# Retention attention and an ELU feed-forward layer: all steps of every engine in a new written order

## The chip, the cores and the metric

The kernel runs on one core of a Trainium2 chip. The core has a matrix engine (TensorE, PE in the profile, with its weight loads in a row of their own, PEld), a vector engine (VectorE, DVE), a scalar engine (ScalarE, ACT), a general engine (GpSimd, POOL) and a queue engine (SyncE, SP), and 16 DMA engines that move data between the chip's memory (HBM) and the core's buffer (SBUF). TensorE writes its results to a small accumulation buffer (PSUM), from which VectorE and ScalarE read. Each engine runs its own instruction list in the order written, and waits on semaphores for what it needs from the others.

The metric is device time in microseconds (us) for one execution, as the median of some runs. A profile is one execution with a recorder beside it; its span is the time between its first and last instruction.

## The reference, cut to what matters

Four batches, eight heads, 768 positions, 64 features for each head; `x` has 3072 tokens of 512 features and the hidden layer has 2048.

```python
for b in range(12):                        # blocks of 64 positions, one after the other
    intra = (qb @ kb^T) * Dmask            # Dmask[i,j] = lam^(i-j) for i >= j, else 0
    intra = intra @ vb
    inter = (qb * lam^(pos+1)) @ kv_state
    out[block] = intra + inter
    kv_state = lam^64 * kv_state + (kb * lam^(63-pos))^T @ vb
h = x @ w_in                               # x: the attention's output, heads side by side
g = where(h > 0, h, exp(min(h, 0)) - 1)
return g @ w_out
```

Inputs and output are fp32; products take fp16 operands and gather in fp32.

## The kernel before, in words

**Tiling.** Work is cut into 24 attention *steps*: step s is block s//2 of the batch pair 2*(s%2) (`where`, L50), that is 128 tokens and eight heads. Steps s and s+2 belong to the same pair of batches, so the state of step s is needed by step s+2. Two steps make a *group* of 256 tokens, of which there are 12; a group's attention output `xt` goes through the feed-forward layer.

**One attention step** on TensorE consists of small products of 64x64 operands, which `visit` (L295) issues in a block: the transposes T of k and q (`mm_T`; for the first steps in another form), the scores S (`mm_S`, into `psZ`), the state update U (`mm_U`, into the other half of `psZ`), the inter part I (`mm_I`, the state with the decayed q) and the intra part O (`mm_O`, masked scores with v). One call of `visit(so, us, ss, sx)` can take O of step `so`, U of `us`, S of `ss` and T of `sx`. Around it the other engines do: `att_C` (L233), the copy of the transposes from PSUM to the tile `T`; `att_P` (L225), the scores times the mask, on VectorE; `att_N` (L273), the new state; `att_X` (L262), the copy of the output to `xt`. Three *decays* prepare operands: `decay_v` (L189, tile `vd`, v by a factor for each row), `decay_s` (L198, tile `sd`, the state by its factor) and `decay_q` (L216, tile `qs`, the transposed q by a factor for each column). Each reads and writes SBUF alone, so VectorE or GpSimd can run it; `decay_s` has a form for ScalarE, too. From step 10 on, `dma_T` (L251) lets the DMA transpose k and q on SP's queue into a tile `TD` of two buffers, so that TensorE needn't.

**The feed-forward layer.** `mm1_h` (L420) is a part of the first product, into one of two PSUM banks `psH` (tag `h`). Two forms of the ELU follow: `mm1_e` (L435) with Exp and Relu on ScalarE and then `mm1_g` (L443) on VectorE, or, for later groups, `elu` (L463) with Relu and Exp on ScalarE one after the other and VectorE reading `psH` once more. The second product of steps 0 to 5 is plain (`mm2`, L490; `mm2_o`, L500, copies and stores); for groups from 3 on it is done with seven smaller products instead of eight (`part`, L559, and `product_of`), with sums of the weights (`w_sum`, L515), sums of g (`g_sum`, L525), and copies and additions of the results (`keep` L578, `add` L583, `c2` L587, `store` L568).

**Loads.** k, q and v come in on GpSimd's DMA queue (`load`, L71), which turns fp32 into fp16 on the way, into 12 buffers each. The issue of such a load is an instruction of GpSimd, and stands in one line with its decays. `wi` (four tiles, `load_wi` L97, two halves each) and `wo` (four, `load_wo` L110) come on the same queue. The second half of `wi2` waits for a semaphore, `crossed`, which TensorE raises after its first inter part. k and q of step 0 come raw as fp32 on other queues (`kraw`, `qraw`) and are cast by `cast0` (L177).

**What sets the order.** Nothing is scheduled by a planner: the pools run under a manual schedule, and every engine has its instructions in the order in which the program writes them. The order is written in three parts: loads ahead of the constants (L130 to L136); the string `start` (L631), whose words are a letter for a function and its arguments (`H0.0.1.0` calls `mm1_h(0, 0, 1, 0)`, `A4.4.5.6` calls `visit(4, 4, 5, 6)`, `R` issues all the later loads up to step 11); and, for groups from 3 on, a loop over eight parts u of each group (L670 to L752) with a tail (L754 to L780). In the loop a part is: one `mm1_h`, then at u of 0 and 4 the next loads, at u of 1 and 5 two decays and one `visit`, then one of the seven products, sums, and the ELU.

## Time and profile before

| what | value |
|---|---|
| time, median of 3 runs | 206.41 us (205.39 to 207.72) |
| profiled execution: span | 204.2 us |
| instructions in the span | 7590 |
| PE (TensorE matmuls) | 189.6 us busy |
| PEld (its weight loads) | 156.6 us busy |
| DVE (VectorE) | 168.7 us busy, 279 instructions |
| ACT (ScalarE) | 146.5 us busy, 283 instructions |
| POOL (GpSimd) | 123.4 us busy, 174 instructions |
| DMA | 24.36 MB in 94194 packets, mean 119 GB/s |

The page gives the span alone; the profiled execution's own time is taken to be what the span and the launch around it make, and 206.41 - 204.2 = 2.2 us is what lies between the span of this one execution and the median of the three.

How to read it: the page gives for each engine the busy time, its share of the span and the number of instructions. A view by stretch gives the same for pieces of the span. A timeline lists instructions by start, each with its start and its length in us, its engine, line, operation, the tile that it writes and those that it reads (`out<-in`), the shapes, and in brackets the idle time before it with what ended it. Groups of instructions carry a count (x22), and three numbers, least, median and largest ns of one. Rows named `POOLq` or `SPq` are issues of a DMA on that engine's queue.

### The profile page before, as it was taken

How to read it: one execution, taken by the hardware profiler on the slowest of the kernel's cores; microseconds unless marked ns; L12 is line 12 of the kernel's file. 1: busy time of each engine (PE TensorE's matmuls, PEld its weight loads, DVE VectorE, ACT ScalarE, POOL GpSimd, SP SyncE). 2: the span in 40 equal slices, each digit the busy share in tenths (PEclk: the TensorE clock that was granted, in tenths of full speed). 3: DMA queues.
4: the chain of work that ended last, by engine and by line, in shares of the span. 5: the costliest groups of instructions: out<-in, count | busy, mean ns of one | idle time of the engine just before them, and what ended most of it. 6: DMA issues, size and time to landing. Idle time of an engine off the chain costs nothing.

```text
span 204.2 us, 7590 instructions
## 1 busy us (share of the span) xinstructions
PE 189.6 (93%) x3216; PEld 156.6 (77%) x3216; DVE 168.7 (83%) x279; ACT 146.5 (72%) x283; POOL 123.4 (60%) x174
## 2 busy tenths in 40 slices
PE   0679899999999999999999989999999999999991
PEld 0457777647777777888888878888888888888881
DVE  4776996489989998999989999989979866758672
ACT  5626987635774879999878677788688788876820
POOL 8977832598998959997709999999222200020000
PEclk9999999999999999999999999999999999999998
DMA  6999999999999999999999999999915404004043
GB/s 102 157 171 171 152 206 196 180 124 156 117 148 150 173 108 172 153 134 78 74 163 109 206 105 86 185 111 105 169 27 69 94 0 108 0 6 100 3 103 103
DMA packets 94194, 24.36 MB, mean 119 GB/s; under 512 B 86160, under 2 KB 91152, under 8 KB 94160
## 3 DMA queue, kind: packets, MB, share of 16 engines
q0 software_dynamic: 73744, 13.64, 94.7%
q1 hardware_dynamic: 19968, 9.77, 26.9%
q10 hardware_dynamic: 448, 0.46, 1.0%
q8 instruction: 25, 0.41, 0.9%
q14 instruction: 9, 0.07, 0.1%
HBM read 27.27 MB, written 6.29 MB: 164 GB/s over the span
## 4 chain that ended last, share of the span: by engine, by line
PE 85%; DVE 4%; DMA 3%; POOL 3%; issue 2%; ACT 1%; POOLq 0%; DVEq 0%
PE psH L428 40%; PE psM L551 23%; PE psM L495 10%; DMA wi<-in_moe_w_in_dram 3%; PE psO_None L328 2%; POOL vn L79 1%; PE psZ L352 1%; PE psO_None L337 1%; PE psHB L551 1%; PE psHA L551 1%; DVE s L533 1%; PE psZ L344 1%; DVE g L475 1%; POOL kn L79 1%; PE psO L359 1%
## 5 line engine op out<-in xcount | busy, mean ns | idle before, releaser
L428 PE MATMUL psH<-xt,wi 128*128 128x256 f16 (+1 forms) x896 | 100.1, 261 | 1.9 <-ACT e L438 0.6
L428 PEld LDWEIGHTS <-wi 128*128 128x128 f16 x896 | 78.2, 100 | 13.3 <-issue 2.1
L475 DVE SCALAR_TENSOR_TENSOR g<-e,psH 128x512 f16<-128x512 f32 x58 | 39.6, 683 | 14.3 <-ACT e L474 13.8
L472 ACT ACTIVATE r<-psH 128x512 f32<-128x512 f32 x58 | 34.7, 598 | 18.3 <-PE psH L428 18.2
L474 ACT ACTIVATE e<-r 128x512 f32<-128x512 f32 x58 | 36.5, 630 | 1.8
L79 POOL DMA_DIRECT2D kn<-in_k_dram x46 | 32.2, 720 | 9.2 <-DMA wo<-in_moe_w_out_dram 5.1
L79 POOL DMA_DIRECT2D vn<-in_v_dram x48 | 34.1, 741 | 2.0 <-DMA wi<-in_moe_w_in_dram 1.1
L438 ACT ACTIVATE e<-psH 128x512 f32<-128x512 f32 x38 | 22.8, 601 | 14.7 <-PE psH L428 14.4
L551 PEld LDWEIGHTS <-s 128*128 128x128 f16 x288 | 28.1, 98 | 3.3
L445 DVE SCALAR_TENSOR_TENSOR g<-e,r 128x512 f16<-128x512 f32 x38 | 25.7, 685 | 4.1 <-ACT r L440 4.0
L220 POOL TENSOR_TENSOR qs<-TD,powi 128x512 f16<-128x512 f16 x11 | 13.9, 1264 | 19.3 <-PE psO_None L328 13.1
L79 POOL DMA_DIRECT2D qn<-in_q_dram x36 | 25.3, 735 | 0.0
L551 PE MATMUL psM<-wt,s 128*128 128x256 f16 x192 | 24.9, 273 | 0.0
L495 PE MATMUL psM<-wo,g 128*128 128x512 f16 x96 | 24.0, 379 | 0.0
L440 ACT ACTIVATE r<-psH 128x512 f16<-128x512 f32 x38 | 22.9, 602 | 0.0
L551 PEld LDWEIGHTS <-g 128*128 128x128 f16 x216 | 20.6, 98 | 2.6
L193 DVE TENSOR_TENSOR vd<-vn,rev 128x512 f16<-128x512 f16 x22 | 17.2, 783 | 1.8 <-DMA vn<-in_v_dram 1.7
L228 DVE TENSOR_TENSOR P<-psZ,mask 128x512 f16<-128x512 f32 x24 | 16.4, 684 | 2.0 <-PE psZ L344 1.1
L551 PE MATMUL psM<-wo,g 128*128 128x256 f16 x136 | 17.6, 272 | 0.0
L495 PEld LDWEIGHTS <-g 128*128 128x128 f16 x96 | 8.7, 98 | 7.0
L570 POOL DMA_DIRECT2D out_dram<-o x2 | 1.1, 574 | 21.1 <-DVE o L585 21.1
L533 DVE TENSOR_TENSOR s<-g 128x1024 f16<-128x1024 f16 x18 | 13.8, 764 | 0.0
(85 smaller groups left out, 228.7 us busy)
## 6 DMA issues: line engine op xcount, KB each, us to landing
out_dram<-o SPq DMA_DIRECT2D x43, 128.0 KB, 3.3
vn<-in_v_dram POOLq DMA_DIRECT2D x48, 64.0 KB, 5.0
kn<-in_k_dram POOLq DMA_DIRECT2D x46, 64.0 KB, 4.3
qn<-in_q_dram POOLq DMA_DIRECT2D x36, 64.0 KB, 4.5
wi<-in_moe_w_in_dram POOLq DMA_DIRECT2D x8, 256.0 KB, 8.9
wo<-in_moe_w_out_dram POOLq DMA_DIRECT2D x4, 512.0 KB, 12.6
qn<-in_q_dram POOLq DMA_DIRECT2D x5, 128.0 KB, 5.3
kraw<-in_k_dram SPq DMA_DIRECT2D x2, 128.0 KB, 4.7
```

Source lines behind the costliest of these rows:

```text
L79: nc.gpsimd.dma_start(out=keep[s][half(r)], in_=src[b + r, :, c * L : (c + 1) * L, :].rearrange("h p d -> p h d"),)
L193: eng.tensor_tensor(out=st[s]["vd"][:], in0=vn[s][:], in1=rev[:].unsqueeze(2).broadcast_to([128, H, D]), op=ALU.mult,)
L228: nc.vector.tensor_tensor(out=d["P"][:].rearrange("p y j t -> p y (j t)"), in0=psS, in1=mask[:].rearrange("p y j t -> p y (j t)"), op=ALU. ...
L428: nc.tensor.matmul(psH[:, i, :], lhsT=wi[n // 4][:, kk, (n % 4) * 128 : (n % 4 + 1) * 128], rhs=xt[grp][:, kk, c0 * 128 : c0 * 128 + T], s ...
L438: nc.scalar.activation(e[:], psH[:], AF.Exp)
L440: nc.scalar.activation(r[:], psH[:], AF.Relu)
L445: nc.vector.scalar_tensor_tensor(out=place(grp, c0, nc_, n0, nb, step), in0=e[:], scalar=-1.0, in1=r[:], op0=ALU.add, op1=ALU.min,)
L472: nc.scalar.activation(r[:], psH[:], AF.Relu, scale=-1.0)
L474: nc.scalar.activation(e[:], r[:], AF.Exp, scale=-1.0)
L475: nc.vector.scalar_tensor_tensor(out=place(grp, 0, 2, u, 2, NF2), in0=e[:], scalar=-1.0, in1=psH[:], op0=ALU.add, op1=ALU.max,)
L495: nc.tensor.matmul(acc[s], lhsT=g_of(s, n), rhs=wo[n // 4][:, n % 4, :], start=(n == 0), stop=(n == NFT - 1),)
L551: nc.tensor.matmul(to, lhsT=lhsT, rhs=rhs, start=start and n == 0, stop=stop and n == NF2 - 1, skip_group_check=True,)
```

## The change

No product, no load and no store is added or taken away. All that is written in three parts before, the loads, `start`, and the loop with its tail, now stands in one string `plan`, in a new order; so each engine's list is in a new order, GpSimd's loads and SP's transposes and stores among it. What else differs:

- words can end in a flag that names the engine. With it, `decay_v` and `decay_s` and `decay_q` (`V`, `D`, `Q`) run on GpSimd instead of VectorE: 30 decays in all, against 19 before. `mm1_e`/`elu_e` (`E`, `e`) take the Relu (or the minimum with 0) on VectorE instead of ScalarE, and `att_X`, `keep` and `mm2_o` copy on VectorE; `att_C` can copy k on ScalarE or q on VectorE.
- `elu` is cut in two words, `e` (Relu and Exp) and `g` (VectorE's combination), which can stand apart.
- the second half of `wi2` no longer waits for `crossed`. TensorE still raises it.
- the loads stand each at its own place (`l`, `w`, `y`), q1 and k1 first; q3 stands ahead of the first `wi`, q4 and k4 ahead of the last `wo`; the stores (`o`) too, one of them (`o18.5`) on GpSimd's queue.
- k of step 0 is cast ahead of q (`Fk Fq`), and the mask product (`K0`) stands later.
- which of the two banks `M` a plain second product takes is listed (`BANK`).

```diff
+    plan = (
+        "Fk Fq A...0 C0.1.1 lq1 lk1 lv0 lv1 K1 A..0. lq3 w0.0 V0 A.0.. A...1 K0 w0.1 lv2 lk2 lq2 "
+        "V1 lk3 P0 C1 A0... A..1. P1 X0 H0.0.1.0 E0.0.1.0 N0 A.1.. w1.1 V2 w1.0 D2 G0.0.1.0 N1 "
+        "A1... X1 A...2 C2.1 H0.1.1.0 D3 E0.1.1.0 A.2.2. A...3 C3.1 H0.0.2.4 Q2 lv3 P2 lq4 w2.0 "
+        "w2.1 lk4 V3.1 y0 G0.1.1.0 I2 A2... N2 Q3.1 X2.1 E0.0.2.4 H0.0.2.6 A.3.3. w3.1 w3.0 y1 "
+        "E0.0.2.6.1 y2 P3 H1.0.1.0 E1.0.1.0.1 H1.0.1.4 I3 y3 G0.0.2.6 E1.0.1.4.1 A3... G1.0.1.4 "
+        "X3 H1.0.1.8 E1.0.1.8.1 H0.0.2.8 E0.0.2.8 A...4 H0.0.2.10 H1.1.1.4 M1.0 G1.0.1.0 "
+        "E1.1.1.4 C4.0.1 A..4. M0.0 lq5 lk5 H0.0.2.14 G0.0.2.8 G1.0.1.8 H0.0.2.12 H1.1.1.0 lv4 "
+        "E0.0.2.10.1 G0.0.2.4 H1.0.2.12 M1.4 M0.4 G0.0.2.10 E0.0.2.14.1 H1.0.2.14 E0.0.2.12.1 "
+        "B1.1 G0.0.2.14 E1.1.1.0 G1.1.1.0 H1.1.1.8 lq6 M0.8 G0.0.2.12 Q4 E1.0.2.12 B1.0 M1.8 "
+        "M1.12 N3 D4 E1.1.1.8.1 M0.12 Z1 P4 B2.0 G1.1.1.8 B4.0 V4 Z0 G1.1.1.4 M2.0 E1.0.2.14.1 "
+        "A...5 M3.0 M2.4 C5 Q5 G1.0.2.12 lk6 lk7 A4.4.5.6 X4 B2.1 G1.0.2.14 M3.4 N4 lq7 lv5 lv6 "
+        "V5 H2.0.1.4 M3.8 E2.0.1.4 G2.0.1.4 P5 C6.1 H2.0.1.12 H2.0.1.8 V6 A5.5.6.7 lk8 M3.12 "
+        "M2.8 X5 P6 H2.1.1.4 H2.0.1.0 E2.0.1.8.1 M2.12 D6 B3.1 H2.1.1.12 Q6 lv7 lk9 H2.1.1.8 V7 "
+        "E2.0.1.12 C7 E2.1.1.4 lk10 lq8 lq9 D5 lv9 lq10 T10 N5 E2.0.1.0 Z2 E2.1.1.8 G2.0.1.0 "
+        "A6.6.7.8 M4.0 E2.1.1.12 G2.0.1.8 D7 P7 H2.1.1.0 B4.1 N6 C8.1 Q7 Z3 lv8 G2.0.1.12 M4.4 "
+        "M4.8 A7.7.8.9 lv10 lv12 X6 Q8 M4.12 E2.1.1.0 X7 h3.0 h3.1 C9.1 G2.1.1.4 G2.1.1.8 "
+        "G2.1.1.12 Z4 G2.1.1.0 N7 M5.0 M5.4 h3.4 h3.2 P8 V8 A8.8.9. h3.5 h3.7 lv11 M5.8 lk11 "
+        "D9.1 lq13 Q9 e3.1 g3.1 e3.0 h3.3 lq11 lk12 D8 e3.4 g3.0 V9 g3.4 lq14 lq12 P9 N8 "
+        "A9.9.10. e3.2 e3.5 X8 g3.2 V10.1 B3.0 lk14 T11 D10 T12 h3.6 lv14 lk13 lk18 M5.12 e3.7 "
+        "e3.3 V11.1 Q11.1 N9 T13 X9 P10 g3.7 lv13 e3.6 Q10 lk15 V14.1 h4.2 e4.2 g3.5 h4.4 g3.6 "
...
+        "o19.0 k10.u2 s10.3 h11.7 g11.5 p10.7 e11.6.1 e11.7 k10.c45.1 p10.3 g11.6 g11.7 j p11.1 "
+        "p11.4 k11.u1 s11.1 a10.2 p11.5 o20.0 s11.2 p11.6 s11.3 p11.2 k11.c45 c10 o21.0 k11.u2 "
+        "p11.7 s11.4 a11.3 o22.1 c11 o23.3 o18.5 p11.3 a11.2 o22.2 "
+    )
...
-            if (i, c) == (2, 1):
-
-                ins.wait_op(crossed, 1, "sem-ge")
...
+    def copy(eng, out, in_):
+        if eng is nc.scalar:
+            nc.scalar.copy(out=out, in_=in_)
+        else:
+            eng.tensor_copy(out, in_)
...
-    def mm1_e(grp, c0, nc_, n0):
+    def mm1_e(grp, c0, nc_, n0, on_dve=0):
         psH, nb, T, name = unit[grp, c0, nc_, n0]
         e = msb.tile([128, nb, T], FP32, tag="e", bufs=4, name=f"e{name}")
         nc.scalar.activation(e[:], psH[:], AF.Exp)
         r = msb.tile([128, nb, T], FP16, tag="r", bufs=4, name=f"r{name}")
-        nc.scalar.activation(r[:], psH[:], AF.Relu)
+        if on_dve:
+            nc.vector.tensor_scalar_max(r[:], psH[:], 0.0)
+        else:
+            nc.scalar.activation(r[:], psH[:], AF.Relu)
         unit[grp, c0, nc_, n0] = (e, r, nb, T, name)
...
-    def elu(grp, u):
-
+    def sbuf_form(grp, u):
+        return grp == 3 or grp == 4 and u < 6
+
+    def elu_e(grp, u, on_dve=0):
+
+        if sbuf_form(grp, u):
+            mm1_e(grp, 0, 2, u, on_dve)
+            return
         psH, nb, T, name = unit[grp, 0, 2, u]
-        if grp == 3 or grp == 4 and u < 6:
-            mm1_e(grp, 0, 2, u)
+        r = msb.tile([128, nb, T], FP32, tag="r", bufs=4, name=f"r{name}")
+        if on_dve:
+            nc.vector.tensor_scalar_min(r[:], psH[:], 0.0)
+        else:
+            nc.scalar.activation(r[:], psH[:], AF.Relu, scale=-1.0)
+        e = msb.tile([128, nb, T], FP32, tag="e", bufs=4, name=f"e{name}")
+        nc.scalar.activation(e[:], r[:], AF.Exp, scale=1.0 if on_dve else -1.0)
+        unit[grp, 0, 2, u] = (psH, e)
+
+    def elu_g(grp, u):
+        if sbuf_form(grp, u):
             mm1_g(grp, 0, 2, u, NF2)
             return
-
-        r = msb.tile([128, nb, T], FP32, tag="r", bufs=4, name=f"r{name}")
-        nc.scalar.activation(r[:], psH[:], AF.Relu, scale=-1.0)
-        e = msb.tile([128, nb, T], FP32, tag="e", bufs=4, name=f"e{name}")
-        nc.scalar.activation(e[:], r[:], AF.Exp, scale=-1.0)
+        psH, e = unit.pop((grp, 0, 2, u))
...
-    nacc = [0]
+    BANK = (1, 0, 0, 1, 0, 1)
...
+    def store(s, how):
+        cols = {1: lo, 2: hi}.get(how, slice(0, DM))
+        queues = {2: (nc.scalar, nc.sync), 3: (nc.sync, nc.scalar), 5: (nc.gpsimd,) * 2}.get(how, (nc.sync,) * 2)
         for r in range(2):
-            queues[r].dma_start(out=rows(s, r)[:, cols], in_=o[half(r), cols])
+            queues[r].dma_start(out=rows(s, r)[:, cols], in_=res[s // 2][s % 2][half(r), cols])
...
-    def later_loads():
-        load_wi(2, [1])
...
-    start = (
-        "Fq K0 Fk V0 A...0 C0 A.0.. K1 A..0. P0 A...1 N0 C1 A0... X0 V1 A..1. P1 A.1.. A1... X1 "
-        "N1 D2 H0.0.1.0 D3 E0.0.1.0 A...2 V2 C2 Q2 H0.1.1.0 A.2.2. I2 R P2 E0.1.1.0 A2... "
...
-    for grp in range(3, NG):
-        old, new = grp - 2, grp - 1
-        for u in range(8):
-            mm1_h(grp, 0, 2, u, NF2)
-            s = 2 * grp + 2 + u // 4
...
     steps = {
-        "I": lambda s: visit(s, None, None, None, True), "C": att_C, "P": att_P, "X": lambda s: att_X(s, nc.scalar),
-        "Y": lambda s: att_X(s, nc.vector), "N": att_N, "D": lambda s: decay_s(s, eng=nc.vector), "L": load_step,
-        "V": lambda s: decay_v(s, nc.vector if s < 99 else nc.gpsimd),
-        "Q": lambda s: decay_q(s, nc.vector if s < 10 else nc.gpsimd),
...
+        "I": lambda s: visit(s, None, None, None, True), "C": att_C, "P": att_P,
+        "X": lambda s, e=0: att_X(s, nc.vector if e else nc.scalar), "N": att_N, "D": lambda s, e=0: decay_s(s, eng=by(e)),
+        "d": lambda s, a, b: decay_s(s, range(a, b)), "V": lambda s, e=0: decay_v(s, by(e)),
+        "Q": lambda s, e=0: decay_q(s, by(e)), "H": mm1_h, "E": mm1_e, "G": mm1_g, "M": mm2, "Z": mm2_o,
+        "K": consts, "B": w_sum, "T": dma_T, "h": lambda g, u: mm1_h(g, 0, 2, u, NF2), "e": elu_e,
+        "g": elu_g, "s": g_sum, "p": part_of, "a": sums, "c": c2, "o": store,
     }
...
```

The words of `plan` that stand beside `start`'s: `l` a load, `w` a half of `wi`, `y` a quarter of `wo`; `h`, `e`, `g` the first product and its ELU for groups from 3 on; `p` one of the seven products, `s` a sum of g, `k` a copy out of a bank, `a` and `c` additions, `o` a store, `j` the two last banks, `d` a `decay_s` on ScalarE.

More of the change, by code (lines that the diff above doesn't have):

```diff
@@ L114, in load_wo @@
         )
+    loads = {
+        "l": lambda a: load(a[0], int(a[1:])), "w": lambda a: load_wi(*map(int, a.split("."))),
+        "y": lambda a: load_wo(int(a)),
+    }
     ij = cst.tile([128, L], I32, name="ij")
@@ L267, in att_X @@
         O = st[s].pop("O").rearrange("p r (y t) -> p r y t", y=NHP)
-        if eng is nc.scalar:
-            nc.scalar.copy(out=to, in_=O)
-        else:
-            eng.tensor_copy(to, O)
+        copy(eng, to, O)
     def att_N(s):
```

224 lines of the change are left out of this document (56 added, 168 removed), and 40 rows, old and new, of tables (plan, start).

## The prediction

> **What bounds the kernel now.** I read the page first: the busy shares and the chain that ended last.
>
> ```profile
> span 204.2 us, 7590 instructions
> ...
> PE 189.6 (93%) x3216; PEld 156.6 (77%) x3216; DVE 168.7 (83%) x279; ACT 146.5 (72%) x283; POOL 123.4 (60%) x174
> ...
> PE 85%; DVE 4%; DMA 3%; POOL 3%; issue 2%; ACT 1%; POOLq 0%; DVEq 0%
> ```
>
> TensorE (PE) holds 85% of the chain. The change leaves every matmul in place and only reorders, so it can win no more than PE's idle time. Where is that? The next view gives busy time by stretch (the columns are PE, PEld, DVE, ACT, POOL, granted clock, DMA share, GB/s; the first number after the stretch is its length).
>
> ```profile
> 6.00:13.20 7.20, 4.64 (x136) 3.50 (x136) 5.95 (x11) 3.30 (x10) 6.00 (x10) 1.00 1.61 160
> 13.20:30.00 16.80, 15.64 (x301) 13.34 (x302) 13.73 (x24) 11.58 (x23) 11.32 (x17) 1.00 1.34 175
> 30.00:60.00 30.00, 29.70 (x582) 20.81 (x580) 24.16 (x40) 19.25 (x36) 22.51 (x35) 1.00 1.55 154
> 60.00:90.00 30.00, 30.00 (x566) 23.25 (x565) 29.27 (x48) 24.03 (x51) 27.23 (x40) 1.00 2.14 149
> 90.00:118.00 28.00, 28.00 (x485) 24.45 (x484) 25.59 (x42) 23.27 (x46) 20.41 (x27) 1.00 1.53 126
> 118.00:123.00 5.00, 4.47 (x41) 3.71 (x39) 5.00 (x6) 3.73 (x7) 5.00 (x6) 1.00 1.38 105
> 123.00:200.00 77.00, 77.00 (x1116) 67.51 (x1113) 62.16 (x102) 57.72 (x104) 25.74 (x32) 1.00 0.66 77
> ```
>
> After 13.2 us PE idles 1.16 (to 30 us), 0.30 (to 60) and 0.53 (118 to 123), together 1.99 us, and nothing elsewhere. A new order can earn at most that behind 13.2 us, plus whatever the start gives. At the start PE waits for VectorE (DVE), then for weights:
>
> ```profile
> 5.87 0.57 DVE L181 CAST qn<-qraw 128x512 f16<-128x512 f32 x1 [1.40 <-DMA qraw<-in_q_dram]
> 6.36 0.67 DVE L597 TENSOR_TENSOR mask<-mask,caus 128x512 f32<-128x512 f32 x1
> 6.49 0.64 PE L398 MATMUL psM<-ident,qn 128*64 128x64 f16 x16 [6.49 <-DVE qn L181]
> 7.14 0.43 DVE L181 CAST kn<-kraw 128x512 f16<-128x512 f32 x1
> ...
> 9.24 0.69 DVE L228 TENSOR_TENSOR P<-psZ,mask 128x512 f16<-128x512 f32 x1 [0.54 <-PE psZ L352]
> ...
> 12.13 0.43 PE L344 MATMUL psZ<-vd,kn 64*64 64x64 f16 x16 [0.79 <-DVE P L228]
> ...
> 12.33 0.44 PE L337 MATMUL psO_None<-P,vn 64*64 64x64 f16 x16
> ...
> 13.24 1.89 PE L428 MATMUL psH<-xt,wi 128*128 128x128 f16 x16 [0.47 <-DMA wi<-in_moe_w_in_dram]
> ```
>
> The first big product starts when the first quarter of `wi` has landed, at 13.24 us; all attention of steps 0 and 1 is finished by then.
>
> **Part 1, the start: later.** The new order casts k before q (`Fk Fq`). PE's order still begins with the transposes of q, so they wait for both casts: 7.14 + 0.43 + 0.57 = 8.14 us against 6.49. I let the k cast start at 7.14 as now; it could go earlier only if `kraw` lands earlier, which no row shows. From there to step 0's masked scores VectorE now has four other steps ahead (copy of q, decay of v0, the mask product, decay of v1), about 0.65 each by these rows, after the 0.64 of transposes: 8.1 + 0.64 + 4 x 0.65 = 11.4 us against 9.24. That is still covered by the weights, and costs nothing by itself. But step 1's update and output (rows at 12.13 and 12.33, now run before the weights) come behind the first product `H0.0.1.0`: 0.43 + 0.44, or about 0.6 at the spacing of warm rows below (0.30 each). And the load of q3 has moved ahead of the first `wi` on GpSimd's queue:
>
> ```profile
> vn<-in_v_dram POOLq DMA_DIRECT2D x48, 64.0 KB, 5.0
> ...
> qn<-in_q_dram POOLq DMA_DIRECT2D x5, 128.0 KB, 5.3
> ```
>
> 128 KB at the 160 GB/s of the first stretch is 0.8 us, so the product starts at 14.0. Together +1.4 us; bounds 0 (the weights land no later, and the moved work fills an idle place) and +2.3 (all of both, and one more wait of 0.8 for k2 and q2, whose loads now stand behind those of v2 and the weights).
>
> **Part 2, stalls that go.** PE's idle places after the start, from the same kind of row:
>
> ```profile
> 19.20 0.32 PE L337 MATMUL psO_None<-P,vn 64*64 64x64 f16 x16 [0.38 <-DVE P L228]
> ...
> 24.93 1.03 PE L428 MATMUL psH<-xt,wi 128*128 128x256 f16 x8 [0.63 <-ACT e L438]
> ...
> 32.94 1.05 PE L428 MATMUL psH<-xt,wi 128*128 128x128 f16 x16 [0.30 <-ACT r L440]
> ```
>
> The first waits for step 2's masked scores; the new order puts step 3's transposes and one product between, so it goes. The second waits for ScalarE (ACT) to free one of the two `psH` banks; there, too, attention work now lies between, and some Relu move to VectorE (`E0.0.2.6.1`). The third is a place where a product follows with only one other product between it and the bank that it needs. The new order has two such places (`H1.1.1.0`, `H1.0.2.12`), with the Relu on VectorE beside ScalarE's Exp, so I leave its 0.30. Gain 0.38 + 0.63 = 1.0. Next late behind them would be the weights `wi2` and `wo0`, in front of which the new order puts q4 and k4; I count nothing for them, and up to 0.8 in the upper bound.
>
> **Part 3, GpSimd beside VectorE.** The stall at 118 to 123 us shows what this part aims at:
>
> ```profile
> 119.87 1.23 POOL L220 TENSOR_TENSOR qs<-TD,powi 128x512 f16<-128x512 f16 x1
> 120.08 1.58 DVE L193 TENSOR_TENSOR vd<-vn,rev 128x512 f16<-128x512 f16 x1
> 120.20 1.03 PE L428 MATMUL psH<-xt,wi 128*128 128x256 f16 x8 [0.33 <-DVE g L475]
> ...
> 122.31 0.92 PE L428 MATMUL psH<-xt,wi 128*128 128x256 f16 x7 [0.20 <-DVE g L475]
> ```
>
> A VectorE step with both inputs in SBUF, begun beside a GpSimd decay, ends only when the decay does. Over the run:
>
> ```profile
> L533 DVE TENSOR_TENSOR s<-g x18: 678/684/1649, 84.0 to 196.3; 128x1024 f16<-128x1024 f16 x18
> ...
> L193 DVE TENSOR_TENSOR vd<-vn,rev x22: 678/683/1580, 7.5 to 156.5; 128x512 f16<-128x512 f16 x22
> ...
> L220 POOL TENSOR_TENSOR qs<-TD,powi x11: 1160/1229/1591, 83.5 to 160.4; 128x512 f16<-128x512 f16 x11
> ```
>
> Medians are undisturbed, maxima are not: a collision costs some 0.9 us of VectorE. GpSimd's decays grow from 19 to 30 (ten `vd` from VectorE, one `qs` net), which is 11 x 1.23 = 13.5 us more for GpSimd, while VectorE gives up ten `vd` and takes Relu and copies for about ten of ScalarE's. If each collision is avoided, the whole 0.53 comes back. If the eleven new decays all met such a step, VectorE would lose 11 x 0.9 = 9.9 us, against the 0.73 + 2.41 us that it idles between 60 and 118. An order fixes neighbours on one engine, not the moment between two, so I take half: -0.3. The Trainium skill (GPSIMD Engine Reference, section 4.1, Engine selection) speaks against the move: two-input elementwise work belongs on VectorE, GpSimd being about twice as slow. The trace agrees, 1229 ns against 683; by that rule this part loses where GpSimd's queue is full, which is the rival below.
>
> **Part 4, blocks of 256 instructions.** PE fetches its program in blocks, on a queue of its own:
>
> ```profile
> q8 instruction: 25, 0.41, 0.9%
> ```
>
> 25 blocks for 6432 instructions; 0.9% of 16 engines' 204.2 us is 29.4 us, 1.2 us a block. In the densest stretch, 46 to 62 us, there are four:
>
> ```profile
> q8 instruction: 4, 0.07, 1.6%
> ```
>
> One in 4 us, against 1.2 to fetch, and the stretches above show no idle PE there. An attention step is 128 of PE's instructions; by the durations above no block of the new order runs in less than about 3.4 us. So this part removes nothing: 0, from both sides.
>
> **Part 5, GpSimd's queue and step 11.** From step 10 on, k and q are transposed by DMA. Before, step 11 goes like this (load of q, its k and q transposes, the scores of step 11 on PE):
>
> ```profile
> 61.55 1.56 POOL L79 DMA_DIRECT2D qn<-in_q_dram  x2
> ...
> 67.31 2.21 SPq L256 DMA_TRANSPOSE TD<-kn  x1
> 69.63 1.24 SPq L256 DMA_TRANSPOSE TD<-qn  x1
> ...
> 79.23 0.30 PE L352 MATMUL psZ<-TD 64*64 64x64 f16 x16
> ```
>
> ```profile
> DMA to landing us min/median/max: 3.4/5.0/7.8
> ```
>
> In the new order GpSimd has more in front of q11: the loads of v10, v11, v12 and q13, eight issues of 0.7, and three decays (`vd3`, `qs3`, `sd9`) of 1.23. That is 9.3 us: the issue moves from 61.55 to 70.8 and the second half leaves at 71.5. A load lands 4 to 5 us later (5.0 above), at 75.5 to 76.5. The transpose lands 5.0 after its issue by the last row (3.4 to 7.8): 80.5 to 81.5. PE has done the same products when it reaches step 11 in both orders, so it asks at 79.2 + 0.4 (parts 1 and 2) = 79.6. A stall of about 1.2, with bounds 0 and 4.7; I take 0.8, since `vd3` and `qs3` stand in the first 45 us, where GpSimd mostly waits for landings anyway, and hide there in part. Steps 12 and 13 follow on the same queue, with nothing counted but the upper bound.
>
> **The sum**, on the profiled execution: 204.2 + 1.4 - 1.0 - 0.3 + 0.8 = 205.1 us. Its span is 2.2 us under the median of the runs, 206.41, so the time is 207.3 us. The tail (last product, two additions, stores) keeps its order and counts 0. The shown runs spread over 205.39 to 207.72, so 1% (2.1 us) is about what can be told from no change.
>
> **Rivals.**
> *Faster: the new order closes the idle places.* All 1.99 us behind 13.2 go, and parts 1 and 5 stay covered: 204.4 us, just 1.0% below. For it: VectorE at 29.27 of 30 us in the fullest stretch is relieved. Against it: PE is 100% busy in most stretches, so nothing more is to be had.
> *Slower: GpSimd's queue takes over.* Place: steps 11 to 13, 75 to 95 us. GpSimd is at 27.23 of 30 us from 60 to 90, and the extra decays stand in front of the loads that the transposes wait for. If q11 issues after 72 us, step 11 loses 3 us (an upper landing) and steps 12 and 13, with transposes gated by the buffers of 10 and 11, about 0.8 each: 207.3 - 0.8 + 4.6 = 211.1 us. It decides at a transpose landing after 79.6; before that it costs nothing.
> *It does not do what it says.* The blocks cost nothing now and decays drift against VectorE's steps as before; the start evens out: 206.4 us.
>
> **How the numbers follow.** Forecast 207.3: 0.40. Faster rival: 0.20. Slower rival: 0.27. No effect: 0.13. The forecast's own terms reach from 205.5 (start 0) to about 209.0. The range takes in most of both rivals: 203.9 to 211.2. Under -1%: nearly all of the faster rival, 0.18. Over +1% (208.5): the slower rival and a tenth out of the forecast, 0.37. The rest, 0.45, lies within 1%.
>
> **What would show it.** Part 1: PE's first matmul near 8.1 us and the first `psH` product near 14.0. Part 2: no wait of over 0.3 us for `P` or `e` between 18 and 26. Part 3: fewer `s` steps over 1.4 us and no idle PE near 120. Part 4: 25 blocks, no idle PE at their edges. Part 5: the scores of step 11 waiting on the q transpose. Wrong would be: `kraw` landing well before 7 us (the start then costs nothing), the q11 issue near 62, or small VectorE waits all along, which this sum has no term for.

## The result, and the profile after

The new order takes 218.93 us (median of 4 runs, 216.07 to 219.85) against 206.15 for the kernel before: a ratio of 1.0582, 95% interval 1.0491 to 1.0674, so 5 to 7% slower. The forecast was 207.3 with a range up to 211.2: wrong. The ratio, like those further on, leaves out runs of over 1.5% above the fastest of their kernel, here the profiled one, the slowest of the four with 219.85 us at a span of 218.1. So 1.75 us lie around a span, not the 2.2 that were added.

The profile page of the new kernel, span, busy shares, the chain that ended last, and the queue of program blocks:

```profile
span 218.1 us, 7591 instructions
...
PE 193.4 (89%) x3216; PEld 158.2 (73%) x3216; DVE 182.4 (84%) x286; ACT 140.6 (64%) x265; POOL 135.2 (62%) x185
...
q8 instruction: 25, 0.41, 0.8%
...
PE 48%; DVE 11%; POOL 8%; issue 3%; DMA 2%; ACT 1%; DVEq 0%; POOLq 0%
```

TensorE's part of the chain falls from 85% to 48%, and VectorE and GpSimd stand in it with 11% and 8%. VectorE is busy for 13.7 us longer with seven instructions more. Where TensorE stands still, by stretch (columns as in the prediction):

```profile
60.00:90.00 30.00, 27.73 (x578) 20.57 (x576) 29.94 (x40) 23.12 (x44) 26.88 (x38) 0.97 1.71 125
90.00:118.00 28.00, 24.16 (x380) 20.27 (x378) 26.66 (x37) 18.95 (x39) 18.32 (x24) 0.97 0.95 82
```

Between 60 and 118 us, where it did not idle at all before, TensorE now idles 2.27 + 3.84 = 6.1 us. The two spans differ by 13.9 us: beside these 6.1, TensorE idles 1.8 us more from 6 to 30, 0.5 more from 30 to 60, 2.1 more from 123 to 200 and 0.5 less from 118 to 123, and its matmuls are busy for 3.8 us longer. VectorE is busy for 29.94 of 30 us with 40 instructions, where it had 48 before: each takes longer. TensorE's waits name it, too (engine, line, what was waited for, total, times, longest):

```profile
PE psM L443 <- DVE qn L223: 8.0, 1, 8.0
PE psH L473 <- DVE g L534: 4.3, 4, 1.6
PE psM L609 <- DVE g L493: 2.3, 1, 2.3
PE psH L473 <- DVE r L486: 2.2, 2, 1.7
PE psM L443 <- DMA qn<-in_q_dram: 1.4, 1, 1.4
...
PE psZ L397 <- ACT T L277: 0.7, 1, 0.7
```

The first row is the start's wait for the cast, also there before (6.5). Three of the others wait for VectorE, 8.8 us together. Which of its instructions are long? The groups by line of the new kernel (busy time and mean ns behind the bar):

```profile
L493 DVE SCALAR_TENSOR_TENSOR g<-e,r 128x512 f16<-128x512 f32 x38 | 31.9, 863 | 1.2 <-ACT r L488 1.1
L591 DVE TENSOR_TENSOR s<-g 128x1024 f16<-128x1024 f16 x18 | 15.9, 890 | 0.1
L235 DVE TENSOR_TENSOR vd<-vn,rev 128x512 f16<-128x512 f16 x12 | 9.5, 790 | 1.5 <-DMA vn<-in_v_dram 1.5
L591 DVE TENSOR_TENSOR s<-s,g 128x1024 f16<-128x1024 f16 x9 | 8.8, 977 | 0.1
L591 DVE TENSOR_TENSOR s<-g,s 128x1024 f16<-128x1024 f16 x9 | 7.1, 791 | 0.1
L253 DVE TENSOR_TENSOR sd<-st,lamL 128x512 f32<-128x512 f16 x9 | 7.0, 779 | 0.0
```

All six have two inputs in SBUF, and undisturbed they take 682 to 686 ns (means of the version without GpSimd's reads, below). Their excess over 683 is 38 x 180 + 18 x 207 + 12 x 107 + 9 x 294 + 9 x 108 + 9 x 96 ns = 16.3 us. The same sum for the kernel before, from its groups, is 18 x 81 + 9 x 91 + 9 x 81 + 22 x 100 ns = 5.2 us, and almost none of it in `g<-e,r`:

```profile
L445 DVE SCALAR_TENSOR_TENSOR g<-e,r 128x512 f16<-128x512 f32 x38 | 25.7, 685 | 4.1 <-ACT r L440 4.0
L193 DVE TENSOR_TENSOR vd<-vn,rev 128x512 f16<-128x512 f16 x22 | 17.2, 783 | 1.8 <-DMA vn<-in_v_dram 1.7
L533 DVE TENSOR_TENSOR s<-g 128x1024 f16<-128x1024 f16 x18 | 13.8, 764 | 0.0
L533 DVE TENSOR_TENSOR s<-s,g 128x1024 f16<-128x1024 f16 x9 | 7.0, 774 | 0.0
L533 DVE TENSOR_TENSOR s<-g,s 128x1024 f16<-128x1024 f16 x9 | 6.9, 764 | 0.0
```

In the traces 19 steps with two inputs in SBUF take over 0.85 us in the new kernel, and 8 in the kernel before. The same sum is 13 us for the version with the old start and 15 us for the one with three state decays on ScalarE, both further on. So the remaining 13.7 - 11.1 = 2.6 us of VectorE are plain work.

The worst stretch of the new kernel in the timeline, VectorE and GpSimd beside each other:

```profile
82.19 2.76 POOL L133 DMA_DIRECT2D kn<-in_k_dram  x4
82.42 6.11 DVE L493 SCALAR_TENSOR_TENSOR g<-e,r 128x512 f16<-128x512 f32 x4
84.87 1.54 POOL L235 TENSOR_TENSOR vd<-vn,rev 128x512 f16<-128x512 f16 x1
86.38 1.59 POOL L262 TENSOR_TENSOR qs<-TD,powi 128x512 f16<-128x512 f16 x1
88.45 1.52 DVE L591 TENSOR_TENSOR s<-g 128x1024 f16<-128x1024 f16 x1
90.01 2.31 DVE L591 TENSOR_TENSOR s<-s,g 128x1024 f16<-128x1024 f16 x1
90.66 1.10 POOL L235 TENSOR_TENSOR vd<-vn,rev 128x512 f16<-128x512 f16 x1
95.96 2.71 DVE L493 SCALAR_TENSOR_TENSOR g<-e,r 128x512 f16<-128x512 f32 x1
96.89 1.22 POOL L262 TENSOR_TENSOR qs<-TD,powi 128x512 f16<-128x512 f16 x1
```

Four steps that need 2.5 us take 6.11, and TensorE stands from 84.75 to 87.02 for one of these `g`. The step at 90.01 ends at 92.32, that is 0.56 after the decay that ended at 91.76; the one at 95.96 ends at 98.67, again 0.56 after the decay's 98.11. Undisturbed steps follow each other by 0.6 us, so it looks as if the VectorE step began its real work when GpSimd's instruction was over.

### The profile page after: what moved, and what is told of

Same layout as the page of the kernel before. It is cut to its first block, busy times and chain, and to the rows that moved or that the text cites. A ratio compares the mean times of both kernels' runs of the same rounds, so it can differ in the third digit from the quotient of the medians.

```text
span 218.1 us, 7591 instructions
## 1 busy us (share of the span) xinstructions
PE 193.4 (89%) x3216; PEld 158.2 (73%) x3216; DVE 182.4 (84%) x286; ACT 140.6 (64%) x265; POOL 135.2 (62%) x185
## 4 chain that ended last, share of the span: by engine, by line
PE 48%; DVE 11%; POOL 8%; issue 3%; DMA 2%; ACT 1%; DVEq 0%; POOLq 0%
PE psH L473 23%; PE psM L609 19%; POOL qn L133 2%; DVE g L493 2%; POOL kn L133 2%; DMA vn<-in_v_dram 2%; DVE s L591 2%; PE psO_None L373 1%; PE psHB L609 1%; PE psHA L609 1%; DVE g L534 1%; DVE st L326 1%; POOL vd L235 1%; DVE sd L253 1%; POOL vn L133 1%
## 5 line engine op out<-in xcount | busy, mean ns | idle before, releaser
L524 ACT ACTIVATE r<-psH 128x512 f32<-128x512 f32 x56 | 33.4, 597 | 22.0 <-PE psH L473 21.9
L133 POOL DMA_DIRECT2D vn<-in_v_dram x48 | 33.4, 732 | 2.0 <-DMA wi<-in_moe_w_in_dram 1.8
L493 DVE SCALAR_TENSOR_TENSOR g<-e,r 128x512 f16<-128x512 f32 x38 | 31.9, 863 | 1.2 <-ACT r L488 1.1
L609 PEld LDWEIGHTS <-g 128*128 128x128 f16 x216 | 21.3, 99 | 5.4 <-DVE g L493 2.5
L553 PE MATMUL psM<-wo,g 128*128 128x512 f16 x96 | 23.2, 380 | 0.0
L253 POOL TENSOR_TENSOR sd<-st,lamL 128x512 f32<-128x512 f16 x8 | 8.7, 1095 | 19.6 <-DVE st L326 19.6
L488 ACT ACTIVATE r<-psH 128x512 f16<-128x512 f32 x27 | 16.1, 597 | 0.0
L591 DVE TENSOR_TENSOR s<-g 128x1024 f16<-128x1024 f16 x18 | 15.9, 890 | 0.1
L553 PEld LDWEIGHTS <-g 128*128 128x128 f16 x96 | 8.7, 98 | 8.2 <-issue 0.3
L326 DVE TENSOR_TENSOR st<-psZ,sd 128x512 f16<-128x512 f32 x20 | 13.6, 680 | 0.4 <-PE psO_None L373 0.4
```

What stands on the lines that cost most here:

```text
L133: nc.gpsimd.dma_start(out=keep[s][half(r)], in_=src[b + r, :, c * L : (c + 1) * L, :].rearrange("h p d -> p h d"),)
L488: nc.scalar.activation(r[:], psH[:], AF.Relu)
L493: nc.vector.scalar_tensor_tensor(out=place(grp, c0, nc_, n0, nb, step), in0=e[:], scalar=-1.0, in1=r[:], op0=ALU.add, op1=ALU.min,)
L524: nc.scalar.activation(r[:], psH[:], AF.Relu, scale=-1.0)
L553: nc.tensor.matmul(acc[s], lhsT=g_of(s, n), rhs=wo[n // 4][:, n % 4, :], start=(n == 0), stop=(n == NFT - 1),)
L591: nc.vector.tensor_tensor(out=gs[grp, i][:], in0=a, in1=b, op=ALU.add if i == 1 else ALU.subtract)
```

## The experiments

Times are medians; ratios are to the kernel before, run on the same chip beside each, since chips differ by some tenths of a per cent. Theory A throughout: GpSimd's decays, which read SBUF, shut out VectorE's two-input steps, and VectorE has no slack to absorb it. The rivals were that the moved work itself, GpSimd's queue, or the start of the new order is what costs.

**One: take away the reads, keep GpSimd's time.** In the new kernel, a decay of v on GpSimd becomes two fills:

```diff
+        if eng is nc.gpsimd:
+            for _ in range(2):
+                eng.memset(st[s]["vd"][:], 0.0)
+            return
```

> The new kernel in which the ten decays of v on GpSimd are replaced by two fills of the same tile with zero (the states of those steps are left out of the result). GpSimd has about the same length of work in the same places, but reads nothing from SBUF. Theory A, in the form that GpSimd's read is what shuts out VectorE's second input: the long VectorE steps beside vd go, 211 to 215. Theory B (a full GpSimd queue makes later decays and loads late): nothing changes, 217 to 220.

Measured: 210.16 us, ratio 1.0224 (1.0173 to 1.0275). A pair of fills takes 1.17 to 1.20 us on GpSimd, a decay 1.07 (median), so its line is as full as before (busy for 134.8 us, 135.2 before), and still 1.0582 - 1.0224 = 3.6%, some 7.4 us, come back, a little more than A had. But fills alone don't wait for v to land. So a copy of one column of v was added behind them:

```diff
+    def stand_in(out, fill, src):
+        for _ in range(2):
+            nc.gpsimd.memset(fill, 0.0)
+        nc.gpsimd.tensor_copy(out, src)
...
+        if eng is nc.gpsimd:
+            stand_in(st[s]["vd"][:, 0, 0:1], st[s]["vd"][:], vn[s][:, 0, 0:1])
+            return
```

> The new kernel with the ten decays of v on GpSimd replaced by two fills of the tile and a copy of one column of v (the states of those steps are left out of the result). Unlike the run with fills alone (210.2), GpSimd still waits for v's landing before it goes on. Theory A (the read of SBUF beside VectorE is what costs): as with fills alone, 209 to 212. Theory B (the wait for v, with loads and other decays queued behind it, is what costs): back to 216 to 220.

Measured: 214.98 us, 1.0420 (1.0352 to 1.0488), between the two theories. TensorE stands still little between 60 and 90 us (29.66 of 30 busy), but 4.1 us from 123 to 200: the 20 decays that still read met other steps, and one `s<-g,s` took 3.03 us. Taking a read away shifts the others, so a part of the reads can't be priced this way. Hence all of them at once, qs and sd in the same manner:

```diff
+        if eng is nc.gpsimd:
+            stand_in(st[s]["sd"][:, 0, 0, 0:1], st[s]["sd"][:], state[s - NPR][:, 0, 0, 0:1])
+            return
...
+        if eng is nc.gpsimd:
+            stand_in(st[s]["qs"][:, 0, 0, 0:1], st[s]["qs"][:], st[s]["T"][:, 1, 0, 0, 0:1])
+            return
```

> The new kernel with all 30 decays on GpSimd replaced by two fills and a copy of one column (so their factors are left out of the result): GpSimd keeps the length of its work and its waits, but VectorE meets no read of it. What is left is the worth of the order itself. Theory A (collisions are all that the new order loses behind the start): 206 to 208, the start's 1 to 2 us above the kernel before. Theory B (the order loses in other ways, too): 209 or more, as with the ten fills.

Measured: 207.34 us, 1.0066 (1.0033 to 1.0099), in A's range. The same stretches and the same groups by line:

```profile
60.00:90.00 30.00, 30.00 (x667) 23.33 (x665) 28.34 (x48) 25.08 (x50) 26.07 (x44) 1.00 1.82 129
90.00:118.00 28.00, 28.00 (x428) 24.66 (x427) 24.45 (x43) 23.09 (x45) 25.69 (x51) 1.00 1.19 109
```

```profile
L507 DVE SCALAR_TENSOR_TENSOR g<-e,r 128x512 f16<-128x512 f32 x38 | 25.1, 683 | 1.6 <-ACT r L502 1.6
L605 DVE TENSOR_TENSOR s<-g 128x1024 f16<-128x1024 f16 x18 | 12.2, 684 | 0.1
```

GpSimd is busy for 25.7 to 26.1 us in each stretch, no two-input step is disturbed, and TensorE idles nowhere between 60 and 118. The same was done to the 19 decays of the kernel before:

> The kernel before with its 19 decays on GpSimd replaced by two fills and a copy of one column (their factors are left out of the result), as was done to the new kernel, which then took 207.3. It tells what GpSimd's reads cost in the old order, and so what each order is worth without them. Theory A (the old order meets few such reads; only the idle 0.5 us at 118 to 123 and some of TensorE's slack come back): 204 to 205.5, so the new order by itself is 2 to 3 us slower. Theory B (the old order pays, too, and the new order by itself is the better one): 203 or less would be needed for the old order to have much to gain, and 207 or more would make the new order the equal or better one.

Measured: 204.93 us, 0.9944 (0.9912 to 0.9975), in A's range. With that the loss splits. The reads cost the new order 1.0582 - 1.0066 = 5.2%, 10.6 us, and the old order 0.6%, 1.2 us. The order without reads is 1.0066 / 0.9944 = 1.2% slower, 2.5 us. By the intervals of the ratios the 10.6 holds to about 2 us, the other two to about 1. Of some 12 us, some nine are the reads. Theory A holds, and the order itself gains nothing. One thing more differs in these versions: fills don't wait for their input, so after a late landing a stand-in is done sooner than a decay. That doesn't explain the gain, for the lists of waits of the new kernel and of the kernel before name no instruction that waits for a decay of GpSimd.

**Two: the two engines alone.** Kernels without the reference's work, with VectorE and GpSimd starting together. V is a VectorE step like `decay_v`, P one like `att_P`, G a decay on GpSimd, F two fills, K two loads:

```diff
+    for phase in ['VVVVVVVV', 'VGVGVGVGVGVGVGVG', 'VFVFVFVFVFVFVFVF', 'VVVVVVVVVVKKKK', 'VVVVVVVVVVVVVVVVKKGKKGKKG', 'PGPGPGPGPGPGPGPG', 'VVVVVVVV']:
+        meet()
+        for w in phase:
+            fns[w]()
```

Each engine runs its own letters in order; `meet` makes both start together by small copies.

> Nothing of the reference is computed: seven phases, each with both engines started together. VectorE runs 8 to 16 steps like the decay of v (two inputs in SBUF), in turn alone, beside 8 decays on GpSimd, beside 8 pairs of fills, beside 8 loads issued by GpSimd, beside loads and decays in turn; then 8 steps with one input in PSUM beside 8 decays; then alone. Theory A (GpSimd's read shuts out VectorE's second input until it ends): spacing 0.6 alone, beside fills, beside loads and with one input in PSUM; 1.5 or more, ending 0.56 after a GpSimd instruction, beside decays. Theory B (any GpSimd work beside it slows it, loads too): over 1.0 beside loads or fills as well.

VectorE's steps and GpSimd's line beside them, phase by phase (decays, fills, loads, loads and decays in turn, and PSUM input beside decays):

```profile
7.36 4.90 DVE L59 TENSOR_TENSOR vo<-x,rev 128x512 f16<-128x512 f16 x8
7.51 4.79 POOL L97 COPY c<-b 128x8 f32<-128x8 f32 x1 [4.27 <-DVE b L96]
12.35 8.03 POOL L59 TENSOR_TENSOR go<-y,rev 128x512 f16<-128x512 f16 x8
...
20.54 4.90 DVE L59 TENSOR_TENSOR vo<-x,rev 128x512 f16<-128x512 f16 x8
...
29.82 6.10 DVE L59 TENSOR_TENSOR vo<-x,rev 128x512 f16<-128x512 f16 x10
...
36.34 14.81 DVE L59 TENSOR_TENSOR vo<-x,rev 128x512 f16<-128x512 f16 x16
...
51.15 4.86 DVE L69 TENSOR_TENSOR po<-psZ,mask 128x512 f16<-128x512 f32 x8
51.45 8.04 POOL L59 TENSOR_TENSOR go<-y,rev 128x512 f16<-128x512 f16 x8
```

Beside fills, beside loads, and with one input in PSUM, a VectorE step has its 0.6 us. Beside loads and decays in turn, 16 steps take 14.81 us instead of 9.7: 5.1 us for three decays. The trace has six steps of 1.52 to 1.55 us there instead of 0.68, 0.85 more each: one beside each decay, ending 0.55 us after it, and one beside the loads ahead of it. Beside decays alone the outcome is the reverse of what was expected: VectorE had begun first, ran its eight steps undisturbed, and GpSimd's small copy and its decays stood until it was done. A second kernel varied this:

```diff
+    for phase in ['PPPVVVVVVVVVVVVGGGGGG', 'VVVVVVVVVVVVVVVVKGKGKGKG', 'VVVVVVVVVVVVVVVVVVVVKKKKGKKKKG', 'VVVVVVVVVVVVVVVVKKFKKFKKF', 'VVVVVVVVVVVVVVVVKKKKKK', 'VVVVVVVV']:
```

> Nothing of the reference is computed; VectorE and GpSimd alone, started together, in six phases. In the last run of this kind a decay behind loads made two VectorE steps long, one beside the decay and one beside the loads ahead of it, while loads by themselves made none long. Here VectorE's two-input steps run beside six decays that GpSimd begins first, beside one pair of load issues and a decay in turn (four times), beside four pairs and a decay (twice), beside two pairs and two fills (three times), beside six pairs, and alone. Theory A (each decay behind loads costs two steps of 0.87 us, however many loads): lengths 16 x 0.6 + 8 x 0.87 = 16.6 us in the second phase, 20 x 0.6 + 4 x 0.87 = 15.5 in the third, 9.8 in the fourth and fifth. Theory B (the loads ahead hold VectorE off as long as a decay waits behind them): the third phase is the worst for each decay, over 18 us.

```profile
4.46 11.00 DVE L59 TENSOR_TENSOR vo<-x,rev 128x512 f16<-128x512 f16 x12
...
15.46 9.71 DVE L59 TENSOR_TENSOR vo<-x,rev 128x512 f16<-128x512 f16 x16
...
35.12 15.51 DVE L59 TENSOR_TENSOR vo<-x,rev 128x512 f16<-128x512 f16 x20
...
50.62 9.71 DVE L59 TENSOR_TENSOR vo<-x,rev 128x512 f16<-128x512 f16 x16
...
62.92 9.72 DVE L59 TENSOR_TENSOR vo<-x,rev 128x512 f16<-128x512 f16 x16
```

The third phase (two decays behind eight loads each) has the 15.5 us of theory A, two long steps for each decay; fills behind loads and loads alone cost nothing. The second phase missed: 9.71 instead of 16.6, since there GpSimd was kept out for the whole burst of VectorE.

**Three: give the work to another engine.** First the ten decays of v back to VectorE (these words alone, out of the string):

```diff
-V3.1 V10.1 V11.1 V14.1 V13.1 V15.1 V17.1 V19.1 V21.1 V20.1
+V3   V10   V11   V14   V13   V15   V17   V19   V21   V20
```

> The new kernel with its ten decays of v back on VectorE, all else as it is; 20 decays stay on GpSimd, about as many as before the change. Theory A (collisions): the 8 us that TensorE loses between 73 and 108 us come from GpSimd's decays standing beside VectorE's steps with two inputs in SBUF, each of which then ends 0.56 us after the GpSimd instruction. Without vd10, vd11 and vd14 in that stretch at least half of the loss goes: 212 to 215 us, with at most four such steps over 1.4 us between 80 and 100, against eight. Theory B (VectorE is too full): the moved steps return as work of 0.6 us each to an engine that is busy for 29.9 of 30 us from 60 to 90, so the time is the same or longer: 219 to 222.

Measured: 219.55 us, 1.0670 (1.0608 to 1.0732): no gain, as B had it, though the reads are fewer. Two rows tell why:

```profile
PE psH L471 <- DVE g L532: 4.9, 5, 3.0
...
145.00 1.40 DVE L233 TENSOR_TENSOR vd<-vn,rev 128x512 f16<-128x512 f16 x1 [2.44 <-DMA vn<-in_v_dram]
```

In the new order `vd17` stands where GpSimd would wait for v17. On VectorE that wait of 2.44 us holds up the ELU behind it, and TensorE waits 3.0 us in one piece. Between 60 and 118 it idles 3.5 us instead of 6.1, so about half came back there, as A had it, and was lost later: from 123 to 200 it idles 4.2 us, against 2.1 in the new kernel. Then three state decays of VectorE's to ScalarE:

```diff
-D5     D7     D8
+d5.0.4 d7.0.4 d8.0.4
```

> The new kernel with three state decays (steps 5, 7 and 8, which VectorE runs between 60 and 80 us) on ScalarE, as the form for ScalarE has it. Theory A (VectorE is the bound from 60 to 95, and each step or collision there counts in full): 3 x 0.6 and one collision of 0.9 go, 2.7 us or more, 214 to 216.5. Theory B (TensorE or GpSimd's loads are the bound there and VectorE only follows): 218 to 220.

Measured: 219.96 us, 1.0695 (1.0639 to 1.0751): A missed. The time is in B's range, but not for B's reason, since TensorE's longest wait, 5.3 us, is for VectorE's `g<-e,r`. The next two-input steps moved up into the place that came free and met more reads; four `g<-e,r` from 82.92 on took 8.06 us together. Then three decays of v from GpSimd to ScalarE, with `v` for a new function:

```diff
-V10.1 V11.1 V14.1
+v10   v11   v14
+        for h in range(H):
+            nc.scalar.activation(st[s]["vd"][:, h, :], vn[s][:, h, :], AF.Copy, scale=rev[:, h : h + 1])
```

> The new kernel with the decays of v of steps 10, 11 and 14, which GpSimd runs between 78 and 92 us, on ScalarE, eight instructions each. Unlike putting them back on VectorE (219.6), this takes the reads from GpSimd without giving VectorE work. Theory A (the reads beside a VectorE without slack cost the 8 us): half of it or more comes back, 212 to 215. Theory B (a decay taken from GpSimd costs as much wherever it goes, here as 2.5 us of ScalarE each): 217 to 220.

Measured: 217.30 us, 1.0539 (1.0473 to 1.0604), as B had it, and within the intervals no change from the new kernel's 1.0582. Long VectorE steps grew fewer, but TensorE now waited for ScalarE, 2.5 us for its Relu and 1.4 us for its copy to `xt`. From 60 to 90 us VectorE, ScalarE and GpSimd are busy for 26.1, 26.6 and 26.4 of 30 us. So it isn't enough that a decay leaves GpSimd: three engines are nearly full there.

**Four: the moved decays in the old order.** The kernel before with the ten decays of v on GpSimd:

```diff
     def decay_v(s, eng):
+        if s in (3, 10, 11, 13, 14, 15, 17, 19, 20, 21):
+            eng = nc.gpsimd
```

> The kernel before with only this changed: the same ten decays of v (3, 10, 11, 13, 14, 15, 17, 19, 20, 21) run on GpSimd instead of VectorE, in the old order. Theory A (collisions cost, wherever the decays stand): each new decay that meets a two-input VectorE step costs it 0.9 us; some half of ten meet one, TensorE waits for part of it: 208 to 213. Theory B (it was the order, not the engine): VectorE is relieved by 7 us and the time stays at 205 to 207.

Measured: 250.24 us, 1.2151, far outside both. It is one wait, in the words of the trace:

```profile
PE psZ L346 <- POOL vd L195: 39.9, 1, 39.9
```

In the old order the decay of step 3 is written behind `R`, all the later loads, and GpSimd ran them first. Without that one (no 3 in the list):

> The kernel before with nine decays of v (10, 11, 13, 14, 15, 17, 19, 20, 21) on GpSimd, without the one of step 3, which in the old order stands behind all the later loads and alone cost 40 us. Theory A (collisions cost also in the old order): by the growth behind that place in the run with ten, 3.4 us above the kernel before, 208 to 210. Theory B (the old order has room for them): 205 to 206.5.

Measured: 210.31 us (207.46 to 212.96), 1.0102 (1.0031 to 1.0174). By its ratio the move costs the old order 2 us: a cost, where B had none, but less than the 3.4 us of A.

**Five: the start.** The new kernel with the words and first loads of the kernel before up to step 2, and then all its own words that are left, in their order:

```diff
-Fk Fq A...0 C0.1.1 lq1 lk1 lv0 lv1 K1 A..0. lq3 w0.0 V0 A.0.. A...1 K0 w0.1 lv2 lk2 lq2 ...
+Fq K0 Fk lv0 lk1 lq1 lv1 w0.0 w0.1 lk2 lq2 lv2 w1.0 w1.1 lk3 lq3 V0 A...0 C0 A.0.. K1 ...
```

> The new kernel with the start of the kernel before: the order of all words up to the transposes and scores of step 2, and the order of the first loads up to q3. From there on the new order. Theory A1 (the start's loss stands for itself): TensorE's lead of about 3.3 us at 25 us comes back and all that follows keeps its length: 214 to 216. Theory A2 (the new order is fitted to moments, and the late start shifts GpSimd's line against VectorE's, so that the collisions at 82 to 98 follow from it): far more comes back, 205 to 210.

Measured: 218.33 us, 1.0624 (1.0570 to 1.0678): neither; nothing came back. TensorE's first product is at 6.5 again, but it then waits 2.3 us for the load of q3, and near 90 us 4.9 us in one piece for a Relu on VectorE. Without the reads, where a small change can be seen (and `lq4` behind `lk4`):

> The new kernel without GpSimd's reads (all 30 decays as two fills and a copy of one column, their factors left out of the result, 207.3 so far) and with the start of the kernel before, q4 loaded behind k4 as before. Theory A (what the new order loses without the reads, 2.4 us against the old order without them, is lost at the start: the first product, the landings of q2 and of the weights): 204.5 to 205.8. Theory B (the early call for step 3's transposes, which stays, and the later load order cost it): 206.5 to 208.

Measured: 207.69 us, 1.0106 (1.0012 to 1.0199), against 1.0066 without the old start: in B's range. Again one wait is in the place of the old ones:

```profile
PE psM L455 <- DMA qn<-in_q_dram: 2.7, 1, 2.7
```

The new order calls for step 3's transposes three blocks earlier. So they were put back, too:

```diff
-A.2.2. ... A...3 C3.1 H0.0.2.4 ... I2 A2... N2 Q3.1
+A.2.2. ... H0.0.2.4 ... I2 A2... N2 A...3 C3.1 Q3.1
```

> The last run of the new kernel without GpSimd's reads and with the start of the kernel before (207.7), in which the transposes of step 3 and their copy now stand three blocks later, behind the output and the new state of step 2, as in the kernel before. TensorE waited 2.7 us there for q3's landing. Theory A (that wait is what is left of the start's loss): 205 to 206, near the old order without reads (204.9). Theory B (another wait of the same load queue takes its place): 206.5 to 208.

Measured: 208.98 us, 1.0168 (1.0070 to 1.0265), above both ranges: that wait is gone, others of 0.3 to 0.8 us for VectorE and ScalarE are there. Where TensorE falls behind is seen: from 6 to 60 us it is busy for 3.72 + 14.29 + 29.37 = 47.4 us in the new order without reads, and for 4.90 + 15.85 + 29.70 = 50.5 in the old one without them. Of these 3.1 us, 1.8 are one gap: at 25 us TensorE stands for 1.78 us before the last four of a product's 32 matmuls and waits for nothing that the profile shows. The version with three decays of v on ScalarE has a gap of 1.28 us at the same place, the new kernel none. In all three one block of TensorE's program is fetched between 23 and 27 us; whether that is the cause isn't shown. The last version has no such gap, is busy for 48.9 us from 6 to 60, and was still no faster. Which words lose the 2.5 us stays open: waits that were taken away made room for others on the loads or the engines behind them.

**Six: a better kernel before?** Two state decays (steps 15 and 16) from GpSimd to ScalarE in the old order, where TensorE idles 0.53 us at 118 to 123:

```diff
     def decay_s(s, places=None, eng=None):
+        if s in (15, 16):
+            eng = None
```

> The kernel before with the state decays of steps 15 and 16 on ScalarE instead of GpSimd: two reads fewer beside VectorE near 115 and 121 us, where TensorE idles 0.5 us, against 2 x 1.3 us more for ScalarE. Theory A (each read taken away from a stretch where VectorE is the bound returns what TensorE waits there): 0.5 to 1.0 us faster. Theory B (ScalarE's Relu and Exp come later by 1.3 us and the bank psH with them): the same or 1 us slower.

Measured: 205.40 us against 205.88, 0.9974 (0.9941 to 1.0007). TensorE is now busy for 5.00 of these 5.00 us, but it idles 0.36 us from 90 to 118 and 0.70 from 123 to 200, where it didn't before, and the gain isn't clear of no change. No version here that computes the whole result beats the kernel before for certain, and by the run without reads there was about 1 us to win.

## Why the prediction was wrong

The two steps that failed are in Parts 3 and 2. The new order was forecast at 207.3 - 206.4 = 0.9 us above the kernel before, and took some 12. Part 3 (-0.3 forecast) missed by 9.7 us, with the reads at 10.6 - 1.2 = 9.4; all the other terms (1.4 - 1.0 + 0.8 = 1.2 forecast) by 1.3, with the order without reads at 2.5.

**What bounds it.** Right, and it held the warning: TensorE had 1.99 us to give back, so the change could win almost nothing and lose much.

**Part 1, the start.** First product 7.98 (8.14 forecast), first big product 13.71 (14.0), the update and output of step 1 behind it: right as far as it went. Missed was q2: its load stood behind those of v2 and k2, which was named for the upper bound only (0.8), and cost 1.4 us.

**Part 2, stalls that go.** They went: no wait for `e`, and 0.2 for `P`. In their place came q2, a wait of 0.7 for the copy of k on ScalarE, and waits for VectorE's Relu. The smaller of the two steps that failed is "Gain 0.38 + 0.63": each stall that goes was counted in full, and what is late next was sought in the weights alone and put at nothing. From 6 to 60 us Parts 1 and 2 had +0.4 us together; the profiles without reads show 3.1 us, of which 1.8 are the gap whose cause is open.

**Part 3, GpSimd beside VectorE.** This is the step that broke the forecast: "I take half: -0.3" for the meetings of GpSimd's decays with VectorE's steps. The mechanism stood there, with its rows, and so did the price of the bad case, 11 x 0.9 = 9.9 us; the measured extra of VectorE is 16.3 - 5.2 = 11.1 us, and the reads cost 10.6 us of the time against 1.2 before. What was wrong is the value taken. Half of eleven collisions is 5 us of VectorE in a stretch where it idles 3.1, so by its own rows the middle was a loss of some 2 us, not a gain. Not known was that a decay behind loads makes two long steps, not one. Nor was VectorE relieved: it gives up ten `vd`, a `qs` and four copies of transposes, but takes 13 Relu or minima and nine other copies, 22 steps where the prediction had about ten, and without any reads it is busy for 167.0 us in the new order, 164.2 in the old. Whether the twenty decays that GpSimd had in any case meet more steps in the new order isn't shown: their excess there is some 8 us with the ten others on VectorE, some 5 with fills in their place, and 5.2 in the kernel before. The Trainium skill's page SBUF — State Buffer, section "Who interferes with whom", states the rule that the runs show: a VectorE instruction with two inputs in SBUF contends with a GpSimd one that reads SBUF, and not with one that only writes. The runs agree: fills beside it left means of 682 to 686 ns, decays made single steps of up to 2.71 us.

**Part 4, blocks.** Right for this kernel: 25 blocks as before, and no idle that falls to them. The gap of 1.78 us in the version without reads (Five) leaves open whether the term is always nothing.

**Part 5, step 11.** The landing was right, by luck: the q transpose is issued at 77.17 (75.5 to 76.5 forecast) and takes 4.2 (median, 5.0 before), so 81.4 (80.5 to 81.5 forecast). q11's loads leave by 74.4, some 3 us later than forecast, and a load of q lands in 3.6 us, not 4 to 5. But TensorE asked for it only at 82.77, since it was late itself. The stall of 0.8 did not occur.

**The rivals.** "GpSimd's queue takes over" had the place (75 to 95 us), the sign and the engine, and not the mechanism: no transposes were waited for on TensorE. No rival had the collisions on the other side of zero, though their price stood in its rows; as a rival of its own it would have given 207.3 + 0.3 + 9.9 = 217.5, next to what was measured. That would have been right in its mechanism and lucky in its number, for it gives VectorE none of the 3.1 us that it idled.

**The sums.** Two slips change nothing: the least of the forecast's own terms, "start 0", gives 207.3 - 1.4 = 205.9, not 205.5, and the start's upper bound is 1.4 + 0.8 = 2.2, not 2.3.

## What to carry to other kernels

Count the steps of VectorE that have two inputs in SBUF, and the GpSimd instructions that read SBUF in the same stretch. A meeting costs VectorE some 0.9 us here. Where VectorE has no idle time, most of that becomes kernel time (10.6 us of 16.3 in the new order), and where it has some, little (1.2 of 5.2 in the old). An order written for other moments does not keep the two apart. Before moving work to GpSimd, replace all its reads with fills of the same length: the difference is what they cost. When a value lies between far ends, take the rows' own middle, and give the bad end a rival with its time.

## What the runs showed of the hardware

- Either engine can keep the other waiting, and who does isn't set by who came first. VectorE's burst of 8 steps without a gap held GpSimd's small copy for 4.79 us, one of 16 steps for 9.6. But of eleven such copies beside a burst of these steps, all begun 0.15 or 0.16 us after it, eight took 0.57 or 0.58 us, and three stood to its end. Where GpSimd's decays had begun first, the two took turns, and VectorE's steps ended 1.45 us apart instead of 0.6 until the decays were done (12 steps in 11.00 us instead of 7.3).
- A decay queued behind loads makes a second VectorE step long that lies beside the loads, before the decay's own record begins (three decays: six long steps in 14.81 us; two: four in 15.51). The step at 88.45 in the new kernel lies like that. Loads alone never did it (9.72 us for 16). Why is open; the records of GpSimd are rough.
- When TensorE stands for long, its clock can fall. The granted clock is 0.81 and 0.85 in the two stretches of the new kernel below, 0.53 from 88 to 90 us and 0.62 from 90 to 92, and 1.00 throughout without the reads. It fell after the wait of 2.27 us that ended at 87.02, so that 16 matmuls took 3.10 us instead of 1.91: this wait of VectorE's cost TensorE 1.2 us more than its own length. In the versions above it fell after single waits of 2.3, 2.5, 3.0, 4.9 and 5.3 us, and not after those of 2.7 (the old start without reads) and 2.9 us (the ten fills with a copy), nor after any of up to 1.8 us. During the wait of 39.9 us it is 0.50. The two stretches (columns as above), and TensorE's products before and after the wait:

```profile
85.00:90.00 5.00, 2.98 (x19) 2.32 (x20) 4.97 (x4) 2.67 (x6) 5.00 (x6) 0.81 1.42 85
90.00:95.00 5.00, 3.33 (x41) 2.28 (x42) 4.96 (x6) 1.22 (x3) 5.00 (x8) 0.85 1.71 170
...
80.84 1.91 PE L473 MATMUL psH<-xt,wi 128*128 128x256 f16 x16
...
87.02 0.72 PE L609 MATMUL psM<-wo,g 128*128 128x256 f16 x5 [2.27 <-DVE g L493]
87.57 3.10 PE L473 MATMUL psH<-xt,wi 128*128 128x256 f16 x16
```
